# The first eight weights' words assembled in a PSUM bank instead of SBUF, in a one-core attention and gated-MLP kernel

## The chip, the cores and the metric

The kernel runs on one core of one Trainium2 chip. The metric is the device time of one execution in microseconds (us), median of several runs. TensorE is written PE, VectorE DVE, ScalarE ACT, GpSimd POOL, and SP is the engine that issues most transfers.

## The reference

The inputs arrive as float64-sized words for the weights and float32 for q, k and v. Three blocks follow one another:

```python
scores = scale * np.matmul(q_c, k_c.transpose(0, 1, 2, 4, 3))   # 64x64 chunks, softmax, times v
x = attention output as (B=8, S=576, 512)
h = np.maximum(x @ w_in, 0.0); u, v = h[..., :512], h[..., 512:]
v_s = np.einsum('ts,bsd->btd', w_spatial, layernorm(v)) + b_spatial[None, :, None]
x = (u * v_s) @ w_out
u = x + (x.transpose(0, 2, 1) @ U @ V).transpose(0, 2, 1)
out = u + np.maximum(u @ w_ch1, 0.0) @ w_ch2
```

## The kernel before, in words

**Layout.** Activations lie transposed. Nearly all matrix products are made with float16 pairs: each operand is split into a high and a low float16 part, and three matmuls (hi·hi, hi·lo, lo·hi; `mm3`, lines 149 to 152) accumulate in a PSUM bank. The attention is cut into 36 tiles of 128 rows; the gated block (`gen_moe`) goes once per batch, eight times; the channel block (`gen_ch`) goes over nine slices of 512 rows.

**The weights.** They come as 44 blocks of 128x512 eight-byte words and are unpacked on the chip, block n in these steps:

- `dec_load` (line 157) issues the transfer of the raw words, for the first eight blocks into buffers called `room` that other tiles use later.
- `dec_abs` (line 163) takes a float32 tile `dt` and has ACT write the scaled high words into it (line 173). Blocks under 12 use the SBUF tag `hid`, which has three buffers.
- `dec_bits` (line 176) works on `dt` in place with three DVE instructions over 128x512 elements: a shift (line 180, one tensor input), an OR with the shifted low words (line 181) and an OR with the sign bit (line 184). Lines 181 and 184 have two tensor inputs each, the raw words and `dt`.
- `dec_parts` (line 188) casts `dt` to the high float16 part on ACT (line 191), and POOL subtracts to make the low part (line 192). The `dt` buffer is free after that.

Blocks 4, 5, 6, 7 (the second half of `w_in`) and then 0, 1, 2, 3 (the first half) are unpacked first, by `gen_dec(0)`; `gen_dec(1)` then unpacks the spatial weights, blocks 8 to 11 and U and V. The other 32 blocks follow later between the other work.

**The opening.** `gen_first` does the first nine attention tiles in float32: scores (line 516), maximum, subtraction and exponential (lines 385 to 389), normalisation (lines 394 to 397), a transpose on PE (line 529), a copy on ACT (line 530), the product with v (line 537), and the split into float16 parts (`a_out`: line 410 on ACT, line 411 on DVE). PE also runs two groups of 16 matmuls whose results nobody uses, one on the tile `warm` (line 451) and one on `idle` (line 465). POOL clears some buffers with memsets (line 897 clears two of them), some of them after block 7 is unpacked. The gated block of batch 0 begins with products of the first attention rows with blocks 4 to 7.

**PSUM.** The pool `ps_h` has three banks with tag `h`. It serves the warm-up matmuls (`wp`), later every product of the gated block (`pb`) and the hidden rows of the channel block (`phid`). The opening's attention uses other banks.

**What sets the order.** The program is written as Python generators that are drained in a fixed order: tiles 0 to 4, then `gen_dec(0)`, `gen_dec(1)`, then batch 0 with parts of batch 1. When the program is built, a scheduler lays the instructions of every engine into one queue, by its own estimate of when each one's inputs and buffers are ready, and puts in the waits. On the chip each engine takes its queue strictly in that order. So a buffer that is thought free earlier can move an instruction in the queue.

Of the kernel before, what the change touches and what calls it, by code (L numbers as in the profile page):

```python
# [8 lines left out]
F32 = mybir.dt.float32  # L9
F16 = mybir.dt.float16  # L10
U32 = mybir.dt.uint32
I64 = mybir.dt.int64
ACTF = mybir.ActivationFunctionType
ALU = mybir.AluOpType
# [87 lines left out]
def moe_kernel(  # L102
# [16 lines left out]
    sb = ctx.enter_context(tc.tile_pool(name="sb", bufs=1))  # L119
    ps_acc = ctx.enter_context(tc.tile_pool(name="ps_acc", bufs=1, space=PSUM))  # L120
    ps_h = ctx.enter_context(tc.tile_pool(name="ps_h", bufs=3, space=PSUM))
# [33 lines left out]
    stage = {}  # L155
# [6 lines left out]

    def dec_abs(name, g=None):
        st, cols = stage[name]
        if isinstance(name, int) and name < 12:
            t = sb.tile([128, 2, 512], F16, tag="hid", name="dt", bufs=3)
            t = t.rearrange("p a n -> p (a n)").bitcast(F32)
        else:
            t = sb.tile([128, 512], F32, tag="o", name="dt", bufs=2)
        if g is not None:  # L170
            nc.scalar.copy(out=t[0:1, 0:1], in_=g[0:1, 0:1])  # L171
        hi = st[:, 0:cols].bitcast(U32)[:, 1::2]
        nc.scalar.activation(out=t[:, 0:cols], in_=hi.bitcast(F32), func=ACTF.Copy, scale=W_SC)
        stage[name] = (st, cols, t)

    def dec_bits(name):
        st, cols, t = stage[name]
        w = st[:, 0:cols].bitcast(U32)
        tb = t[:, 0:cols].bitcast(U32)
        nc.vector.tensor_scalar(out=tb, in0=tb, scalar1=3, scalar2=None, op0=ALU.logical_shift_left)  # L180
        nc.vector.scalar_tensor_tensor(  # L181
            out=tb, in0=w[:, 0::2], scalar=29, in1=tb, op0=ALU.logical_shift_right, op1=ALU.bitwise_or
        )
        nc.vector.scalar_tensor_tensor(  # L184
            out=tb, in0=w[:, 1::2], scalar=0x80000000, in1=tb, op0=ALU.bitwise_and, op1=ALU.bitwise_or
        )

    def dec_parts(name):
# [67 lines left out]
    def gen_dec(part):  # L256
# [17 lines left out]
        def run(names, loaded=False, step=1700.0):  # L274
            n = len(names)
            for i in range(-1, n + 2):
                if i + 1 < n and not loaded:
                    ld(names[i + 1])
                if 0 <= i < n:
                    dec_abs(names[i])  # L280
                if 0 <= i - 1 < n:
                    dec_bits(names[i - 1])
                    fin(names[i - 1])
                yield "wait", step
# [28 lines left out]
    def next_rest(g):  # L313
        i = given[1]
        load_rest(i + 1)
        n = late[i]
        dec_abs(n, g)
        if i == 11:
            load_rest(16, nc.sync)
        elif 12 <= i < 24:  # L320
            load_rest(min(i + 4, 24))
        dec_bits(n)
        dec_parts(n)
        given[1] += 1
# [674 lines left out]
```

## Time and profile before

| | |
|---|---|
| runs before, median (lowest to highest) | 1315.21 us (1314.82 to 1318.34) of 3 |
| span of the profiled execution | 1312.6 us |
| own time of the profiled execution | not listed apart from its span; the median lies 2.6 us above the span |
| busy share of the span: PE, DVE, ACT, POOL | 97%, 41%, 39%, 39% |
| DMA | 81.43 MB, 62 GB/s over the span |

The span runs from the first to the last instruction. An engine is busy while one of its instructions runs; an instruction that is held back after its start counts as busy too, so one kind of instruction at one shape can have very different durations. The idle time in front of an instruction is put down to what ended last before it.

### The profile page before, as it was taken

The page shows a single profiled execution, that of the slowest core. Times are in us where ns is not written, and L with a number is a line of the kernel's source. Part 1 is how long each engine was busy: PE and PEld are TensorE (multiplying, and loading weights), DVE is VectorE, ACT ScalarE, POOL GpSimd, SP SyncE. Part 2 cuts the span into 40 slices and gives each one's busy share as a digit, 9 for nine tenths or more (in the row PEclk, how much of TensorE's full clock was granted, in tenths as well). Part 3 has the DMA queues.
Part 4 walks back from the last instruction along what each step waited for, and adds up shares of the span by engine and source line. Part 5 has one row for each costly group of instructions (what it writes and reads, how often), then busy time and mean ns, then how long its engine had stood idle before and what let it go on. Part 6 is the DMA issues. An engine that isn't in the chain of part 4 may idle for free.

```text
span 1312.6 us, 20572 instructions
## 1 busy us (share of the span) xinstructions
PE 1270.3 (97%) x8324; PEld 727.5 (55%) x8324; DVE 532.3 (41%) x946; ACT 517.3 (39%) x1062; POOL 518.4 (39%) x644
## 2 busy tenths in 40 slices
PE   7899888899999999999999999999999999999998
PEld 5677455445666556654665456645655565544443
DVE  7975787655343533334134514242113211221211
ACT  7865566545545433533344424323122212221110
POOL 7654877656555454534155415223111311020000
PEclk7889999899999999999999999999999999999999
DMA  8644353432224311321024101210011001000000
GB/s 283 194 150 109 104 169 97 136 88 79 61 65 74 92 33 42 75 51 41 4 68 91 49 1 33 40 37 5 0 27 36 8 0 28 18 24 1 32 0 32
DMA packets 99015, 81.43 MB, mean 62 GB/s; under 512 B 73828, under 2 KB 74468, under 8 KB 98920
## 3 DMA queue, kind: packets, MB, share of 16 engines
q1 hardware_dynamic: 97768, 75.92, 21.2%
q10 hardware_dynamic: 1152, 4.19, 1.0%
q8 instruction: 65, 1.06, 0.3%
q14 instruction: 30, 0.25, 0.1%
HBM read 53.62 MB, written 9.44 MB: 48 GB/s over the span
## 4 chain that ended last, share of the span: by engine, by line
PE 73%; DVE 8%; DMA 7%; ACT 6%; POOL 4%; issue 3%; SPq 0%; DVEq 0%; ACTq 0%; POOLq 0%
PE acc L150 8%; PE acc L152 8%; PE acc L151 8%; PE phid L151 8%; PE phid L150 8%; PE phid L152 8%; PE pb L150 7%; PE pb L152 7%; PE pb L151 7%; DMA pt<-ph 2%; DVE dt L184 2%; DMA vf<-in_v_dram 2%; DVE dt L181 1%; DMA st<-in_wk_dram 1%; POOL vbd L376 1%
## 5 line engine op out<-in xcount | busy, mean ns | idle before, releaser
L830 DVE SCALAR_TENSOR_TENSOR hid<-phid,hid 128x512 f16<-128x512 f32 x144 | 99.2, 689 | 383.5 <-ACT hid L828 383.2
L150 PE MATMUL phid<-uT,wch 128*128 128x512 f16 x576 | 219.3, 381 | 0.0
L152 PE MATMUL phid<-uT,wch 128*128 128x512 f16 x576 | 219.1, 380 | 0.0
L151 PE MATMUL phid<-uT,wch 128*128 128x512 f16 x576 | 219.1, 380 | 0.0
L151 PE MATMUL acc<-hid,wch 128*128 128x512 f16 x576 | 218.6, 379 | 0.2 <-DVE hid L830 0.2
L152 PE MATMUL acc<-hid,wch 128*128 128x512 f16 x576 | 218.6, 379 | 0.0
L150 PE MATMUL acc<-hid,wch 128*128 128x512 f16 x576 | 208.1, 379 | 0.7 <-ACT hid L828 0.7
L152 PEld LDWEIGHTS <-wch 128*128 128x128 f16 x1152 | 112.9, 98 | 132.8 <-issue 1.8
L150 PEld LDWEIGHTS <-wch 128*128 128x128 f16 x1152 | 112.9, 98 | 120.3 <-issue 4.5
L151 PEld LDWEIGHTS <-wch 128*128 128x128 f16 x1152 | 113.0, 98 | 116.0 <-issue 1.0
L828 ACT ACTIVATE hid<-phid 128x512 f16<-128x512 f32 x144 | 85.5, 594 | 176.6 <-PE phid L152 175.5
L376 POOL TENSOR_TENSOR vbd<-vf,vbd 64x512 f16<-64x512 f32 x54 | 65.0, 1204 | 113.1 <-ACT vbd L375 99.2
L702 POOL TENSOR_TENSOR gt<-g,gt 128x288 f16<-128x288 f32 x64 | 50.4, 789 | 137.0 <-ACT gt L700 136.6
L363 POOL TENSOR_TENSOR qbd<-qk,qbd 64x512 f16<-64x512 f32 x54 | 64.5, 1195 | 46.9 <-ACT qbd L362 44.9
L751 POOL TENSOR_TENSOR uT<-x,uT 128x512 f16<-128x512 f32 (+7 forms) x64 | 47.7, 756 | 89.4 <-ACT uT L750 86.5
L768 POOL TENSOR_TENSOR tr<-x,tr 128x64 f16<-128x64 f32 x64 | 47.5, 763 | 86.8 <-issue 47.1
L150 PE MATMUL pb<-gt,w 128*128 128x288 f16 x256 | 72.9, 286 | 3.8 <-ACT dt L171 1.9
L150 PE MATMUL pb<-sp_m,vn 128*128 128x288 f16 x256 | 73.5, 287 | 2.9 <-DVE g L697 2.9
L151 PE MATMUL pb<-xT,w 128*128 128x288 f16 x256 | 74.5, 291 | 0.0
L152 PE MATMUL pb<-xT,w 128*128 128x288 f16 x256 | 74.4, 290 | 0.0
L150 PE MATMUL pb<-xT,w 128*128 128x288 f16 x256 | 74.3, 291 | 0.0
L151 PE MATMUL pb<-sp_m,vn 128*128 128x288 f16 x256 | 73.6, 287 | 0.0
(179 smaller groups left out, 2343.9 us busy)
## 6 DMA issues: line engine op xcount, KB each, us to landing
st<-in_wk_dram SPq DMA_DIRECT2D x24, 512.0 KB, 3.6
out_dram<-ot SPq DMA_DIRECT2D x32, 256.0 KB, 2.1
vf<-in_v_dram SPq DMA_DIRECT2D x27, 256.0 KB, 2.7
qk<-in_q_dram SPq DMA_DIRECT2D x27, 256.0 KB, 2.7
qk<-in_k_dram SPq DMA_DIRECT2D x27, 256.0 KB, 3.0
room<-in_wk_dram SPq DMA_DIRECT2D x8, 512.0 KB, 7.2
wch<-in_wk_dram ACTq DMA_DIRECT2D x8, 512.0 KB, 3.2
wch<-in_k_dram SPq DMA_DIRECT2D x9, 256.0 KB, 2.9
```

The costliest lines, as they stand in the source:

```text
L150: nc.tensor.matmul(out=o, lhsT=wh, rhs=xh, start=start, stop=False)
L151: nc.tensor.matmul(out=o, lhsT=wh, rhs=xl, start=False, stop=False)
L152: nc.tensor.matmul(out=o, lhsT=wl, rhs=xh, start=False, stop=stop)
L181: nc.vector.scalar_tensor_tensor(out=tb, in0=w[:, 0::2], scalar=29, in1=tb, op0=ALU.logical_shift_right, op1=ALU.bitwise_or)
L184: nc.vector.scalar_tensor_tensor(out=tb, in0=w[:, 1::2], scalar=0x80000000, in1=tb, op0=ALU.bitwise_and, op1=ALU.bitwise_or)
L363: nc.gpsimd.tensor_tensor(out=qbd[r, 1, :, c, :], in0=qv[r], in1=qbd[r, 0, :, c, :], op=ALU.subtract)
L376: nc.gpsimd.tensor_tensor(out=vbd[r, 1, :, :, c, :], in0=vf[r], in1=vbd[r, 0, :, :, c, :], op=ALU.subtract)
L702: nc.gpsimd.tensor_tensor(out=gt[:, 1, m, c], in0=g, in1=gt[:, 0, m, c], op=ALU.subtract)
L751: nc.gpsimd.tensor_tensor(out=buf[:, 1, m, c], in0=x2[:, m, t], in1=buf[:, 0, m, c], op=ALU.subtract)
L768: nc.gpsimd.tensor_tensor(out=th[:, o0:o0 + n], in0=x2[:, m, t0:t0 + n], in1=th[:, t0:t0 + n], op=ALU.subtract)
L828: nc.scalar.activation(out=hd[:, 0, :], in_=p, func=ACTF.Relu)
L830: nc.vector.scalar_tensor_tensor(out=hd[:, 1, :], in0=p, scalar=0.0, in1=hd[:, 0, :], op0=ALU.max, op1=ALU.subtract)
```

## The change

For blocks under 8, `dec_abs` now takes `dt` from the PSUM tag `h` (a bank of the gated block), and the first two DVE instructions work there in place. The third writes its result into a tile of the SBUF tag `hid`, which is taken only then, and which ACT and POOL read as before. Blocks 8 to 11 and all others stay as they are.

```diff
     def dec_abs(name, g=None):
         st, cols = stage[name]
-        if isinstance(name, int) and name < 12:
+        if isinstance(name, int) and name < 8:
+            t = ps_h.tile([128, 512], F32, tag="h", name="dp")
+        elif isinstance(name, int) and name < 12:
             t = sb.tile([128, 2, 512], F16, tag="hid", name="dt", bufs=3)
             t = t.rearrange("p a n -> p (a n)").bitcast(F32)
         else:
...
         nc.vector.scalar_tensor_tensor(
             out=tb, in0=w[:, 0::2], scalar=29, in1=tb, op0=ALU.logical_shift_right, op1=ALU.bitwise_or
         )
+        to = tb
+        if isinstance(name, int) and name < 8:
+            t = sb.tile([128, 2, 512], F16, tag="hid", name="dt", bufs=3)
+            t = t.rearrange("p a n -> p (a n)").bitcast(F32)
+            to = t[:, 0:cols].bitcast(U32)
+            stage[name] = (st, cols, t)
         nc.vector.scalar_tensor_tensor(
-            out=tb, in0=w[:, 1::2], scalar=0x80000000, in1=tb, op0=ALU.bitwise_and, op1=ALU.bitwise_or
+            out=to, in0=w[:, 1::2], scalar=0x80000000, in1=tb, op0=ALU.bitwise_and, op1=ALU.bitwise_or
         )
```

## Rows read from the trace of the kernel before

**Rows 1.** The page: busy time of PE, and PE's granted clock in 40 slices.

```profile
PE 1270.3 (97%) x8324; PEld 727.5 (55%) x8324; DVE 532.3 (41%) x946; ACT 517.3 (39%) x1062; POOL 518.4 (39%) x644
...
PEclk7889999899999999999999999999999999999999
```

**Rows 2.** Busy time by stretch: us, engines in turn, granted clock, DMA share, GB/s.

```profile
0.00:40.00 40.00, 33.26 (x164) 23.92 (x164) 30.38 (x57) 31.88 (x55) 28.57 (x28) 0.79 0.78 270
40.00:80.00 40.00, 35.64 (x212) 25.83 (x212) 39.09 (x81) 29.79 (x60) 22.93 (x32) 0.83 0.57 181
300.00:600.00 300.00, 298.97 (x2247) 173.09 (x2245) 124.88 (x232) 137.59 (x278) 149.66 (x184) 1.00 0.26 65
```

**Rows 3.** DVE's groups from 7 to 40 us: count, busy us, mean ns, idle before.

```profile
L181 DVE SCALAR_TENSOR_TENSOR dt<-room,dt 128x512 uint32<-128x512 uint32 x8 | 6.8, 846 | 0.1
L184 DVE SCALAR_TENSOR_TENSOR dt<-room,dt 128x512 uint32<-128x512 uint32 x8 | 6.6, 821 | 0.1
L180 DVE TENSOR_SCALAR dt<-dt 128x512 uint32<-128x512 uint32 x8 | 4.9, 615 | 6.9 <-ACT dt L173 6.8
L385 DVE TENSOR_REDUCE mx<-sp 128x8 f32<-128x512 f32 x4 | 2.7, 680 | 0.0
```

**Rows 4.** Timeline of DVE: start, duration in us, instruction, idle before and its releaser.

```profile
9.00 0.69 DVE L184 SCALAR_TENSOR_TENSOR dt<-room,dt 128x512 uint32<-128x512 uint32 x1
9.79 0.43 DVE L180 TENSOR_SCALAR dt<-dt 128x512 uint32<-128x512 uint32 x1
...
25.60 1.31 DVE L180 TENSOR_SCALAR dt<-dt 128x512 uint32<-128x512 uint32 x1
26.83 0.67 DVE L184 SCALAR_TENSOR_TENSOR dt<-room,dt 128x512 uint32<-128x512 uint32 x1
...
29.24 1.09 DVE L184 SCALAR_TENSOR_TENSOR dt<-room,dt 128x512 uint32<-128x512 uint32 x1
33.30 0.68 DVE L180 TENSOR_SCALAR dt<-dt 128x512 uint32<-128x512 uint32 x1 [2.97 <-ACT dt L173]
34.01 1.65 DVE L181 SCALAR_TENSOR_TENSOR dt<-room,dt 128x512 uint32<-128x512 uint32 x1
35.58 0.68 DVE L385 TENSOR_REDUCE mx<-sp 128x8 f32<-128x512 f32 x1
```

**Rows 5.** Timeline of POOL.

```profile
24.81 1.82 POOL L897 MEMSET qbd<- 128x2048 f16 x1
...
28.62 3.83 POOL L192 TENSOR_TENSOR w<-dt,w 128x512 f16<-128x512 f32 x3
32.41 2.69 POOL L232 TENSOR_TENSOR sp_m<-st,sp_m 128x576 f16<-128x576 f32 x2
```

**Rows 6.** Timeline of ACT.

```profile
30.36 0.62 ACT L191 CAST w<-dt 128x512 f16<-128x512 f32 x1 [1.04 <-DVE dt L184]
...
32.61 0.66 ACT L173 ACTIVATE dt<-room 128x512 f32<-128x512 f32 x1
...
38.53 0.57 ACT L652 ACTIVATE rz<-pb 128x512 f32<-128x512 f32 x1
```

**Rows 7.** Timeline of PE.

```profile
28.06 0.63 PE L150 MATMUL pb<-w,xT 128*128 128x512 f16 x1
...
38.21 1.95 PE L537 MATMUL of<-wch 128*128 128x64 f32 x16
41.87 0.39 PE L150 MATMUL pb<-w,xT 128*128 128x512 f16 x1 [1.71 <-ACT xT L410]
...
43.44 1.09 PE L529 MATMUL tp<-ident,wch 128*128 128x128 f32 x4 [0.97 <-DVE wch L397]
```

**Rows 8.** Busy time by stretch, as in rows 2, for two short ones.

```profile
44.00:48.00 4.00, 4.00 (x12) 1.63 (x11) 3.71 (x5) 3.48 (x6) 3.77 (x5) 0.50 0.50 197
66.00:74.00 8.00, 7.99 (x38) 6.21 (x38) 8.00 (x27) 4.97 (x13) 3.59 (x6) 0.57 0.51 169
```

**Rows 9.** Waits of the SP queue, 0 to 100 us: total us, times, longest.

```profile
SPq L160 <- DVE dt L184: 18.7, 7, 9.0
```

## The prediction

> **What bounds the kernel now.** First the page: PE is busy 97% of the span, and its granted clock stays at 0.9 or more outside the first slices and one later one [rows 1]. The stretches then say where PE is short of work. From 300 to 600 us it is busy 298.97 of 300 us at full clock, so nothing that DVE does there can help; in the first 80 us it is busy 68.9 us, at 0.79 and 0.83 of its clock [rows 2]. The eight unpackings lie in the first 40 us. After them, from 40 to 80 us, DVE is busy 39.09 of 40 us [rows 2]: there every microsecond of DVE work saved or moved forward counts, up to what PE can take. PE's fixed work follows behind the opening, so a shift of the opening passes through to the end almost whole.
>
> In the groups of DVE, the three instructions of the eight unpackings take 6.8 + 6.6 + 4.9 = 18.3 us [rows 3]. In the timeline the two-input ones take 0.67 to 0.69 us when undisturbed, the shift 0.43 us; but single ones take 1.31, 1.09 and 1.65 us [rows 4]. Beside each of the long ones POOL has an instruction running: a memset from 24.81 to 26.63, subtractions from 28.62 to 32.45, further ones from 32.41 to 35.1 [rows 5].
>
> The second thing to see is a hole. DVE stands 2.97 us before the shift of the eighth block at 33.30, waiting for ACT's line 173, which began only at 32.61 [rows 4, 6]. Behind that shift, in DVE's queue, stands the maximum of an attention tile (line 385 at 35.58), whose softmax ends in the transpose on PE at 43.44 [rows 4, 7]. ACT for its part had stood 1.04 us before 30.36 for the stretched line 184 [rows 6]. PE then has gaps of 1.71 us before 41.87 and 0.97 us before 43.44 [rows 7]. After them its granted clock is 0.50, the lower of its two levels (1.2 against 2.4 GHz), from 44 to 48 us, with no idle time in that stretch [rows 8].
>
> **The change part by part.**
>
> *The shift, line 180.* It now reads and writes PSUM. Undisturbed it takes 0.43 us in SBUF; DVE's other single-input pass over 128x512 words, the reduction of line 385, reads PSUM and takes 0.680 [rows 3, 4]. I take the slower, 0.69, since PSUM is what it shares with line 385: 8 x 0.69 = 5.5 us against 4.9 now, a loss of 0.6. The lower end is 8 x 0.43 = 3.4, a gain of 1.5. The Trainium skill speaks against the change here: "VectorE: DVE Perf Modes", in "Why PSUM operands drop a tier", says that a PSUM operand takes from such an instruction the mode that reads with both SBUF ports. By it the sum has the loss of 0.6; without it, the gain of 1.5. No run here shows a shift in PSUM.
>
> *The two ORs, lines 181 and 184.* One of their two tensor inputs leaves SBUF. If the stretching beside POOL ends, each costs its undisturbed 0.69: 5.5 us each, against 6.8 and 6.6, a gain of 1.3 and 1.1. If it stays, nothing is gained. The skill's "SBUF — State Buffer", in "Who interferes with whom", says that a DVE instruction with two SBUF inputs contends with a POOL instruction that reads SBUF, and one with at most one such input does not. The long rows beside POOL agree with its first half; of the second half no row tells. By it the gain is whole. No row shows DVE writing PSUM. Above, I bound all three instructions by 0.85, the mean of line 181 as it stands: 24 x 0.85 = 20.4 us, 2.1 more than now.
>
> Sum on DVE: 18.3 - 16.5 = 1.8 us less.
>
> *ACT's line 173.* It writes PSUM instead of SBUF. It takes 0.66 now; ACT reading PSUM at this size takes 0.57 [rows 6]. Eight times 0.09 is 0.7 us to gain at most; since no reason excludes a loss, I allow as much upward, and take none. ACT is busy 31.88 of 40 us, which covers most of it [rows 2].
>
> *The buffers.* This is the larger part. Before, a `hid` buffer was held from line 173 to POOL's line 192. The eighth block needed the fifth one's, whose line 192 is the first of three from 28.62, so done about 29.9, after POOL's memsets [rows 5]. With `dt` in PSUM, line 173 of block eight waits only for a bank, free after line 184 of an earlier block; the sixth one's ended at 27.5 [rows 4]. So ACT can do it before its other work, and the hole of 2.97 us closes but for the new wait: line 184 now takes the `hid` buffer, and for the eighth block still needs the one free at 29.9. Block seven ends at 30.33 now, about 28.5 without the stretches; the eighth's first two steps add 1.2 us; 0.2 to 0.4 of waiting are left. I take 2.97 - 0.4 = 2.6 us.
>
> *PSUM banks.* Three banks are shared with `pb`. The warm-up and eight word tiles come before the first `pb`; taken in turn, it needs the bank of the sixth block, free at 27.5, for its matmul at 28.06 [rows 4, 7]. So 0.5 us cover it; if that is gone, PE waits by as much as line 184 is late.
>
> *SP.* No transfer moves by itself. SP stands 18.7 us in seven waits for line 184 before loads on line 160 [rows 9]; loads that wait for one of the eight can go earlier, and their landing is not what PE waits for in rows 7. I cost it at nothing; cover gone, a load late by a DVE step costs that step, under 1 us.
>
> *The sum.* DVE gains 1.8 + 2.6 = 4.4 us before the saturated stretch. What PE can take: its gaps, 1.71 + 0.97 = 2.7 us, and, if these go and the clock does not fall after them, half of the 4 us at 0.50 and half of the 1.09 us transpose: 2.5 us. That is 5.2 us, more than DVE gives, so DVE decides: 4.4 us. The profiled execution spans 1312.6 us, and 2.6 more make the median of 1315.2: I forecast 1315.2 - 4.4 = 1310.8 us. From 0.3%, or 3.9 us, on a measurement can tell it from no change.
>
> **The rivals.**
>
> *Only the stretches go.* The scheduler leaves line 173 of block eight behind the spatial weights' casts on ACT. For it: ACT's queue is full there. Against: its buffer was what was late. DVE then saves 1.8 us: 1313.4.
>
> *The stretches stay.* What holds the ORs is not their second SBUF input, or POOL holds PSUM work as well. The shift loses 0.6 and the hole closes by little: 1315.8. Against it: undisturbed rows of one line agree within 0.02 us, and only those beside POOL are long [rows 4, 5].
>
> *The wait moves to DVE, and the kernel is slower.* Line 184 of block eight takes the place of line 173 as the one that waits for POOL. Before, ACT's wait left DVE's queue free to pass tiles that stood ahead. If the three steps of block eight now stand at about 27 us in DVE's queue, line 184 stands there until 29.9, with a normalisation and a split of the attention behind it: a stall of 2.9 us, which PE sees as a gap. Another stretch at half clock like the one of rows 8 costs 2.5; half of the saving of 1.8 comes off: 2.9 + 2.5 - 0.9 = 4.5 us, 1319.7. It decides once line 184 stands more than about 2.5 us ahead of POOL. For it: POOL comes to line 192 of block five only at 28.62 [rows 5]. Against it: the scheduler lays POOL's queue too, memsets included, and has other work to put ahead.
>
> **How the numbers follow.** The forecast case gets 0.46, the stretches alone 0.25, the wait on DVE 0.21, stretches that stay 0.08. The forecast case has a range of its own: with gaps gone but the clock still falling it gives 2.7 us (1312.5; 0.04 of the 0.46). At best PE takes all its 5.2, and the later fall, 8 us at 0.57 from 66 to 74 [rows 8], goes too, worth 3.4: 8.6 us, 1306.6. So faster by over 0.3% gets 0.42, within it 0.04 + 0.25 + 0.08 = 0.37, slower 0.21. The range runs from 1306.6 to 1319.8, to just past the slower case; the bound of DVE's unknown price, 2.1 us up, lies inside it.
>
> **What would show it.** Right: lines 181 and 184 of the eight at 0.69 each with POOL busy beside them; the shift at 0.69; the wait of about 3 us before an eighth shift gone, and the maximum of the third tile some 4 us before 35.58; the gaps near 40 to 43 us smaller, and the clock at full after them. Wrong: an idle DVE, or a long line 184, ended by POOL's line 192; ORs still over 1 us beside POOL; or the same gaps and half-clock stretch a little later.

## The result, and the profile after

The changed kernel takes 1323.73 us (median of 6 runs, 1322.22 to 1329.01), the kernel before 1316.24 us in the same comparison (6 runs, 1314.82 to 1318.34). The ratio is 1.0055, with a 95% interval of 1.004 to 1.007: **slower by some 7 us**, where 1310.8 was forecast, and outside the range. The profiled execution took 1323.86 us and spans 1322.1, against 1312.6 before.

Line numbers are 2 to 8 higher than before: the shift is line 182, the ORs are 183 and 192, the cast is 199, the split of an attention tile is 418 on ACT. First the page, PE and its clock in 40 slices, to be held against [rows 1]:

```profile
PE 1271.6 (96%) x8324; PEld 729.5 (55%) x8324; DVE 535.1 (40%) x946; ACT 517.5 (39%) x1062; POOL 513.3 (39%) x644
...
PEclk7799899999999999999999999999999999999999
```

PE is busy 1.3 us longer in a span that is 9.5 us longer, so most of the time went into gaps. The stretches (columns as in [rows 2]) of the changed kernel:

```profile
0.00:40.00 40.00, 33.09 (x161) 24.11 (x162) 29.53 (x60) 32.62 (x57) 30.31 (x30) 0.79 0.83 285
40.00:80.00 40.00, 33.21 (x186) 23.87 (x186) 36.13 (x75) 27.44 (x56) 19.98 (x31) 0.79 0.55 159
300.00:450.00 150.00, 145.35 (x1164) 85.46 (x1161) 63.31 (x115) 72.14 (x144) 81.18 (x99) 1.00 0.28 68
```

and the last of these stretches in the kernel before:

```profile
300.00:450.00 150.00, 149.40 (x1167) 87.23 (x1164) 64.86 (x121) 74.48 (x149) 85.84 (x103) 1.00 0.30 73
```

From 40 to 80 us DVE is busy 3.0 us less than before [rows 2]. It is not relieved, it is short of work: PE did 186 matmuls there instead of 212. And PE lost another 4 us from 300 to 450, hundreds of microseconds after the last instruction that the diff touches.

The steps that the diff does touch did what was expected. DVE's groups from 7 to 40 us, against [rows 3]:

```profile
L182 DVE TENSOR_SCALAR dp<-dp 128x512 uint32<-128x512 uint32 x8 | 5.6, 696 | 2.6 <-ACT dp L175 2.6
L183 DVE SCALAR_TENSOR_TENSOR dp<-room,dp 128x512 uint32<-128x512 uint32 x8 | 5.4, 681 | 0.0
L192 DVE SCALAR_TENSOR_TENSOR dt<-room,dp 128x512 uint32<-128x512 uint32 x8 | 5.4, 679 | 0.2
```

Together they take 16.4 us, where 16.5 was forecast and 18.3 stood before. The timeline of DVE, against [rows 4]:

```profile
27.42 0.68 DVE L183 SCALAR_TENSOR_TENSOR dp<-room,dp 128x512 uint32<-128x512 uint32 x1
28.21 0.69 DVE L192 SCALAR_TENSOR_TENSOR dt<-room,dp 128x512 uint32<-128x512 uint32 x1
31.97 0.69 DVE L393 TENSOR_REDUCE mx<-sp 128x8 f32<-128x512 f32 x1 [3.07 <-PE sp L524]
32.70 0.69 DVE L396 TENSOR_TENSOR wch<-sp,mx 128x512 f32<-128x512 f32 x1
35.57 0.69 DVE L402 TENSOR_REDUCE sm<-wch 128x8 f32<-128x512 f32 x1 [2.18 <-ACT wch L397]
```

The eight blocks are done at 28.9 us. Before, the last OR of the eighth ran to 36.9:

```profile
36.18 0.69 DVE L184 SCALAR_TENSOR_TENSOR dt<-room,dt 128x512 uint32<-128x512 uint32 x1
```

The maximum of the third tile comes at 31.97 instead of 35.58. So DVE won its time, and then stood 3.07 us for PE's scores and 2.18 us for ACT's exponential. ACT's timeline, and then PE's, with its two longest gaps up to 66 us:

```profile
39.74 0.69 ACT L237 ACTIVATE st<-st 128x576 f32<-128x576 f32 x1 [2.49 <-DMA st<-in_wsp_dram]
...
44.83 0.58 ACT L418 CAST xT<-of 128x512 f16<-128x512 f32 x1
```

```profile
37.66 1.95 PE L545 MATMUL of<-wch 128*128 128x64 f32 x16
...
45.47 0.61 PE L150 MATMUL pb<-w,xT 128*128 128x512 f16 x1 [4.57 <-ACT xT L418]
...
63.93 0.47 PE L150 MATMUL pb<-w,xT 128*128 128x512 f16 x1 [2.10 <-ACT xT L418]
```

PE had finished the second tile's product (`of`) at 39.6. Its split, line 418, stands in ACT's queue behind a step of a spatial weight (line 237), whose transfer was issued at 33.73 and took 5.9 us, and behind seven more instructions. PE waits 4.57 us for it; before, the gap at this place was 1.71 us, and the same split ran at 41.23. Behind the gap PE's granted clock stays at the lower level for longer than before, where it was 0.50 from 44 to 48 us [rows 8] and 0.85 from 48 to 52:

```profile
44.00:48.00 4.00, 2.40 (x9) 1.50 (x9) 3.94 (x8) 3.48 (x7) 3.71 (x5) 0.50 0.28 54
48.00:52.00 4.00, 4.00 (x18) 3.35 (x18) 3.48 (x9) 1.64 (x4) 0.69 (x4) 0.50 0.83 259
```

All queues have been laid anew: the rows of PE, DVE, ACT, POOL and SP stand in another order, ACT's and DVE's from about 10 us on, the others' from about 30. PE, DVE, ACT and POOL have their last difference between 475 and 490 us, SP at 314; behind that the order is the old one. The program has the same number of instructions on every engine.

To see where the time goes I use one sum for all kernels: the time elapsed less what PE's matmuls begun by then take at full clock (0.213 us for one of 512 float16 columns, 0.107 us for one of 64 float32 columns, which is the spacing of their starts where the clock is full, and others in proportion to their columns). It is the time that PE has lost, by standing or by half clock, in each profiled execution:

| us lost by PE | 0 to 70 | 70 to 300 | 300 to 450 | 450 to 1300 |
|---|---|---|---|---|
| before | 26.1 | 37.3 | 3.9 | 16.8 |
| changed | 30.3 | 38.9 | 8.4 | 15.9 |

These are single executions. The three kernels of the old order (before, psum_old_order and own_buffers_old_order below) lose 26.1 to 26.5 us up to 70 us and 3.9 to 4.2 us from 300 to 450, but 37.3 to 40.8 us from 70 to 300. So in the second column a difference of 3 us says nothing about the order.

### The profile page after: what moved, and what is told of

Its sections match the earlier page's. It is cut to its first block, busy times and chain, and to the rows that moved or that the text cites. A ratio compares the mean times of both kernels' runs of the same rounds, so it can differ in the third digit from the quotient of the medians.

```text
span 1322.1 us, 20572 instructions
## 1 busy us (share of the span) xinstructions
PE 1271.6 (96%) x8324; PEld 729.5 (55%) x8324; DVE 535.1 (40%) x946; ACT 517.5 (39%) x1062; POOL 513.3 (39%) x644
## 3 DMA queue, kind: packets, MB, share of 16 engines
q1 hardware_dynamic: 97768, 75.92, 21.1%
## 4 chain that ended last, share of the span: by engine, by line
PE 71%; DVE 8%; DMA 6%; POOL 6%; ACT 6%; issue 3%; SPq 0%; DVEq 0%; POOLq 0%; ACTq 0%
PE acc L152 8%; PE phid L151 8%; PE phid L150 8%; PE phid L152 8%; PE acc L151 8%; PE acc L150 8%; PE pb L150 6%; PE pb L152 6%; PE pb L151 6%; DMA pt<-ph 2%; DMA vf<-in_v_dram 2%; DVE dt L192 1%; POOL vbd L384 1%; DVE dt L183 1%; POOL wch L200 1%
## 5 line engine op out<-in xcount | busy, mean ns | idle before, releaser
L150 PE MATMUL pb<-gt,w 128*128 128x288 f16 x256 | 73.6, 288 | 4.1 <-DVE hid L838 4.1
L150 PE MATMUL pb<-sp_m,vn 128*128 128x288 f16 x256 | 73.2, 286 | 1.5 <-DVE g L705 1.5
L151 PE MATMUL pb<-gt,w 128*128 128x288 f16 x256 | 73.5, 288 | 0.0
```

The lines of the kernel that those rows point to most:

```text
L150: nc.tensor.matmul(out=o, lhsT=wh, rhs=xh, start=start, stop=False)
L151: nc.tensor.matmul(out=o, lhsT=wh, rhs=xl, start=False, stop=False)
```

## The experiments

**How an order was forced.** The scheduler keeps any order that dependencies demand. In the runs below, unless said otherwise, each engine's instructions are tied to a given order by dependencies of the scheduler alone, with both ends on one engine and no semaphore; SP's issues are tied as well. In the traces of these runs every engine's rows stand in the order asked for. At the old order the tying costs nothing that can be told (own_buffers_old_order below, ratio 0.9997); at the new order it was not measured by itself. Lines of these kernels are 8 higher again. The code, shortened:

```diff
+    for e, order in ORDER.items():          # one list for each engine
+        for x, y in zip(order, order[1:]):
+            tc.add_manual_dep(traced[e][y], traced[e][x].name, NoSync)
```

**1. The old order with the words in PSUM (psum_old_order), and the new order with the words in SBUF (sbuf_new_order).** The first is the changed kernel with the order of the kernel before, the second the kernel before with the order of the changed one.

> The words stand in PSUM as in the changed kernel, but every engine's queue is pinned to the order of the kernel before. Theory A (the new order of the queues costs the time): 1313 to 1317 us, as the kernel before or 1 to 2 us under it, with the stretched ORs gone. Theory B (the words in PSUM cost it: a slower shift, banks shared with the gated block): 1321 to 1325 us, as the changed kernel.

> The words stand in SBUF as before, but every queue is pinned to the order of the changed kernel. Theory A: 1321 to 1327 us, as the changed kernel or a little worse, since the fourth word tile must now wait on ACT for a buffer in an order that was made for free banks. Theory B: 1314 to 1318 us, as the kernel before.

Measured: 1318.28 us, ratio 1.0014 (1.0003 to 1.0025), and 1327.76 us, ratio 1.0096 (1.0069 to 1.0124). The first lies 1.3 us above the range of theory A and 2.7 under that of B, the second 0.8 us above that of A. With the change, but not its order, nearly all of the loss is gone; with the order, but not the change, it is there in full and more. The lost time shows it at the same places: 26.3 and 4.2 us (0 to 70 and 300 to 450 us) in the first, 32.7 and 7.7 in the second.

In the old order the rows of the three steps are not shorter with the words in PSUM: 18.4 us, against 18.3 before. DVE's groups from 7 to 40 us in psum_old_order:

```profile
L191 DVE SCALAR_TENSOR_TENSOR dp<-room,dp 128x512 uint32<-128x512 uint32 x8 | 6.5, 811 | 0.1
L200 DVE SCALAR_TENSOR_TENSOR dt<-room,dp 128x512 uint32<-128x512 uint32 x8 | 6.4, 798 | 0.1
L190 DVE TENSOR_SCALAR dp<-dp 128x512 uint32<-128x512 uint32 x8 | 5.5, 688 | 7.2 <-ACT dp L183 7.2
...
L411 DVE TENSOR_SCALAR sm<-sm 128x8 f32<-128x8 f32 x2 | 2.4, 1184 | 0.0
L413 DVE TENSOR_TENSOR wch<-wch,sm 128x512 f32<-128x512 f32 x2 | 2.3, 1154 | 0.0
```

and two ORs that are still long, in the timeline of DVE and then of POOL:

```profile
24.11 1.75 DVE L411 TENSOR_SCALAR sm<-sm 128x8 f32<-128x8 f32 x1
24.18 1.68 DVE L200 SCALAR_TENSOR_TENSOR dt<-room,dp 128x512 uint32<-128x512 uint32 x1
24.78 1.67 DVE L191 SCALAR_TENSOR_TENSOR dp<-room,dp 128x512 uint32<-128x512 uint32 x1
```

```profile
24.03 1.80 POOL L913 MEMSET qbd<- 128x2048 f16 x1
```

The instruction that POOL's memset holds is now one of the softmax, over 8 elements, whose operands are in SBUF; it takes 1.75 us and ends with the memset (25.86 and 25.83), and the two ORs queue behind it. The Trainium skill, "SBUF — State Buffer", in "Who interferes with whom", says that a DVE instruction in a mode that uses both port pairs and a POOL instruction lock each other out for the whole of one of them, and that a DVE instruction with at most one SBUF input outside such modes is free of it. This small instruction agrees with the first half. The ORs at 27.42 and 28.21 in the changed kernel, 0.68 and 0.69 us beside two subtractions of POOL, agree with the second:

```profile
26.95 2.27 POOL L200 TENSOR_TENSOR w<-dt,w 128x512 f16<-128x512 f32 x2
```

At the new order, on the other hand, the three steps are short without PSUM too. Their groups in sbuf_new_order (lines 181, 184 and 180 of the kernel before), with the words in SBUF:

```profile
L189 DVE SCALAR_TENSOR_TENSOR dt<-room,dt 128x512 uint32<-128x512 uint32 x8 | 5.7, 716 | 0.0
L192 DVE SCALAR_TENSOR_TENSOR dt<-room,dt 128x512 uint32<-128x512 uint32 x8 | 5.4, 682 | 0.1
L188 DVE TENSOR_SCALAR dt<-dt 128x512 uint32<-128x512 uint32 x8 | 5.0, 623 | 6.6 <-ACT dt L181 6.6
```

That is 16.1 us, against 16.4 in the changed kernel; in own_buffers_new_order below, again in SBUF, it is 17.2. So most of the changed kernel's gain on these steps, or all of it, comes with the order: what POOL does beside an OR depends on it.

**2. Which stretch of the order costs (old_opening_new_rest, new_opening_old_rest).** The words in PSUM; each queue up to 120 us in one order, and then in the other.

> Words in PSUM; the queues follow the kernel before for what it starts in its first 120 us, and the changed kernel's order for the rest. Theory A split in two: the opening's order costs about 4 us and the later order about 5; here the later part alone, 1319 to 1322 us. If the opening alone is at fault: 1314 to 1317 us. Theory B: 1321 to 1325.

> Words in PSUM; the queues follow the changed kernel for what it starts in its first 120 us, and the order of the kernel before for the rest. Theory A split in two: the opening alone, 1318 to 1321 us, with PE's gap of 4.6 us before the split of the second attention tile. If the opening alone is at fault: 1321 to 1325 us. Theory B: 1321 to 1325.

Measured: 1322.98 us, ratio 1.0049 (1.0032 to 1.0065), and 1328.18 us, ratio 1.01 (1.0073 to 1.0127). The lost time by stretch is 25.6, 40.2, 7.7, 16.3 us in the first and 32.0, 49.5, 4.1, 17.1 us in the second. The opening loses where it is the new one, and 300 to 450 us where the rest is the new one. The halves do not add up, though. The second is 7 us above its range, and by the ratios the two cost 0.49% and 1.0%, where the whole new order costs 0.55%. Its 49.5 us from 70 to 300 are more than in any other kernel here; part of that is chance, since the profiled execution, 1333.21 us, is the slowest of its four. What waits there was not followed; the two orders may not fit where they are joined.

**3. Is it the one split on ACT (split_ahead, splits_and_copy_ahead)?** The changed kernel's order; in the first, the split of the second tile stands ahead of the spatial weight that waits for its transfer; in the second, two more steps of the chain stand ahead, ACT's copy of the third tile's transposed scores and DVE's part of the split.

```diff
-ACT: ... 67 (spatial weight, waits for its load) ... 27 (split of the second tile) ...
+ACT: ... 27 67 ...
```

> The changed kernel in its own pinned order, but ACT's split of the second attention tile stands in front of the spatial block whose load is late, instead of eight instructions behind it. Theory C (ACT's queue, standing for that load, is what costs the opening): PE's gap of 4.6 us near 41 to 45 us shrinks to under 1 us and 1 to 4 us of the 7 are won: 1320 to 1323 us. Rival D (the gap is due to PE's or DVE's work and only moves): 1323 to 1325, with another gap of like size behind it.

> As the run before, and also ACT's copy of the third tile's transposed scores and DVE's half of the second tile's split stand in front of the spatial work. Theory C: the whole loss of the opening, about 4 us, is won back: 1318.5 to 1321 us. Rival D: no better than 1323.

Measured: 1325.69 us, ratio 1.0064 (1.0042 to 1.0087), and 1325.76 us, 1.0064 (1.004 to 1.0087). Neither is better than the changed kernel, and both lie above what was expected if ACT's queue were the cause. PE's gap is still there, behind another step each time. PE in split_ahead:

```profile
48.83 3.67 PE L553 MATMUL of<-wch 128*128 128x64 f32 x16 [5.20 <-ACT wch L546]
...
66.52 0.61 PE L158 MATMUL pb<-w,xT 128*128 128x512 f16 x1 [2.47 <-ACT xT L426]
```

and in splits_and_copy_ahead:

```profile
42.52 2.00 PE L553 MATMUL of<-wch 128*128 128x64 f32 x16 [1.18 <-ACT wch L546]
...
49.16 1.09 PE L545 MATMUL tp<-ident,wch 128*128 128x128 f32 x4 [4.65 <-DVE wch L413]
...
64.11 0.61 PE L158 MATMUL pb<-w,xT 128*128 128x512 f16 x1 [2.74 <-ACT xT L426]
```

So the wait that the profile names was not by itself the cause: the chain of an attention tile goes through PE, DVE, ACT and PE again, and with one link moved ahead the next one was late in both runs. What would make the whole chain early in this order is not shown.

**4. Mending the stretch from 300 us (old_order_from_300, both_mended).** The changed kernel's order up to 300 us, then the old one; in the second also the moves of splits_and_copy_ahead.

> The changed kernel in its own pinned order for what it starts in its first 300 us, then the order of the kernel before. Theory E (the later order of the changed kernel loses 4 us more than the old one between 300 and 450 us, where PE stands for the transposes of the softmax): 1318.5 to 1321 us. Rival F (those waits follow from the lateness of the opening, whatever the order): 1323 to 1325 us.

> Both edits: the opening with the three instructions ahead, and the old order from 300 us on. Theories C and E together: 1314.5 to 1317.5 us, level with the kernel before. If one of them fails: 1318.5 to 1321 us.

Measured: 1326.05 us, ratio 1.0055 (1.0034 to 1.0076), and 1327.79 us, 1.0083 (1.006 to 1.0105). Both miss what was expected of them. From 300 to 450 us they lose 9.8 and 9.4 us, no less than the 8.4 of the changed kernel. Rival F, that the lateness of the opening does this, is out as well: in new_opening_old_rest, with the old order from 120 us on behind the same new opening, this stretch loses 4.1 us. So the order from 120 to 300 us has a part in it. What the new order loses there is at least named by the waits of PE from 300 to 450 us, in the changed kernel and then in the kernel before:

```profile
PE o L150 <- DMA pt<-ph: 4.6, 4, 1.8
```

```profile
PE o L150 <- DMA pt<-ph: 0.5, 1, 0.5
```

The late transfers are the transposes of later attention tiles (`pt`). Two other traces, one of each order, agree: 4.3 us in own_buffers_new_order, 0.4 in own_buffers_old_order. Why the transfers are late in this order was not found.

**5. PSUM or the order: the words in buffers of their own (sbuf_words_own_buffers, own_buffers_new_order, own_buffers_old_order).** sbuf_new_order left a doubt: there the words still held the `hid` buffer, so its waits are not the changed kernel's. Here the words lie in two SBUF buffers of their own, and `hid` is taken by the third DVE step alone, as in the changed kernel. The first leaves the order to the scheduler, the other two tie it to that of the changed kernel and to the old one.

```diff
-            t = ps_h.tile([128, 512], F32, tag="h", name="dp")
+            t = sb.tile([128, 512], F32, tag="o", name="dp", bufs=2)
```

> The words of the eight blocks in SBUF, in two buffers of their own (shared with the output's tiles later), with the hid buffer taken only by the third DVE step, as in the changed kernel. Nothing is in PSUM, and the scheduler lays the queues as it likes. If the freed hid buffer is what made the new order and the new order is what costs: the queues come out near the changed kernel's, the opening (to 70 us) loses 4 to 6 us more than before, and the time is 1321 to 1328. If PSUM itself were the cost: 1313 to 1317, no slower than before.

> The words in two SBUF buffers of their own, as in sbuf_words_own_buffers, and every queue in the order of the changed kernel (1323.7 us). Nothing is in PSUM, and no hid buffer is held over the three DVE steps. If the order is the cost: 1322 to 1326, the opening to 70 us loses 4 to 6 us more than before's 26, and PE stands for the ACT split of the second tile near 45 us. If a part of the cost was PSUM: that part is missing, 1316 to 1320.

> The same words in SBUF buffers of their own, and every queue in the order of the kernel before. With the words in PSUM this order took 1318.3 (1.0014 of before). If PSUM is what costs the 0.14%: 1316 to 1317, level with before. If it is chance or the freed buffer: 1318, as with PSUM.

Measured: 1319.53 us, ratio 1.0017 (1.0003 to 1.0032); 1326.84 us, 1.0076 (1.0046 to 1.0105); and 1316.91 us, 0.9997 (0.9978 to 1.0016). The second is the clearest run of the study: no word in PSUM, `hid` taken as in the changed kernel, its order, and the whole loss (0.8 us above the range expected). It loses 32.8 us up to 70 us and 7.9 from 300 to 450. The third says that at the old order nothing is lost; its interval and psum_old_order's overlap, so whether PSUM costs the 0.14% there is open.

The first run missed its expectation in part. The freed `hid` buffer alone, with nothing in PSUM, does make the scheduler lay every queue anew, and the result is slower than before. But it is a third order, not the changed kernel's: its rows differ from those of the kernel before only between 22 and 114 us. Its opening loses 25.3 us, as little as before, and its 300 to 450 us 4.2. Where it loses its 0.17% is not shown: the 40.9 us that it loses from 70 to 300 us are 40.8 in own_buffers_old_order, which is level with the kernel before.

At the old order DVE can be compared with and without PSUM. The same groups as under 1, in own_buffers_old_order:

```profile
L191 DVE SCALAR_TENSOR_TENSOR dp<-room,dp 128x512 uint32<-128x512 uint32 x8 | 6.8, 847 | 0.1
L200 DVE SCALAR_TENSOR_TENSOR dt<-room,dp 128x512 uint32<-128x512 uint32 x8 | 6.6, 819 | 0.1
L190 DVE TENSOR_SCALAR dp<-dp 128x512 uint32<-128x512 uint32 x8 | 4.5, 563 | 7.3 <-ACT dp L183 7.3
...
L411 DVE TENSOR_SCALAR sm<-sm 128x8 f32<-128x8 f32 x2 | 1.8, 902 | 0.0
L413 DVE TENSOR_TENSOR wch<-wch,sm 128x512 f32<-128x512 f32 x2 | 1.4, 680 | 0.0
```

PSUM takes 0.5 us off the ORs, adds 1.0 to the shift and 1.5 to the softmax steps, which now meet POOL instead. The sums, 21.1 us with the words in SBUF and 23.1 with them in PSUM, are not DVE's time, though: rows that wait behind one another cover the same moments, as the three from 24.11 do. With each moment counted once, DVE is busy 26.00 of the 33 us with the words in PSUM, and 26.35 without; psum_old_order first, then own_buffers_old_order, columns as in [rows 2]:

```profile
7.00:40.00 33.00, 26.68 (x143) 20.25 (x142) 26.00 (x51) 28.04 (x50) 19.89 (x18) 0.74 0.77 274
7.00:40.00 33.00, 25.17 (x144) 19.36 (x143) 26.35 (x51) 28.23 (x50) 21.98 (x18) 0.79 0.77 273
```

So at this order PSUM moves DVE's long rows to other instructions and gives it next to nothing.

**6. The step that the forecast rested on (eighth_word_ahead, eighth_word_and_softmax_ahead, own_buffers_softmax_ahead, sbuf_old_order_softmax_ahead).** The forecast's 2.6 us were to come from ACT doing the first step of block eight earlier. In the first run this is the only move in the old order, with the words in PSUM. In the second, the third tile's exponential and the second tile's split stand ahead on ACT as well. The third has this order with the words in SBUF buffers of their own. The fourth is the kernel before with the two softmax moves alone.

```diff
-ACT: ... 59 61 57 60 63 62 56 (first step of block eight) ...
+ACT: ... 56 59 61 57 60 63 62 ...
-ACT: ... 64 58 65 28 (exponential) 92 66 67 203 68 27 (split) ...
+ACT: ... 28 64 58 65 92 66 67 27 203 68 ...
```

> The words in PSUM, every queue in the order of the kernel before (as psum_old_order, 1318.3 us), but ACT's first step of the eighth block stands six places further ahead, before the spatial weights. If the late first step of the eighth block holds the opening back, as the prediction took it: DVE's wait of 2.9 us before the eighth shift closes to under 0.5, the maximum of the third tile comes about 1.4 us earlier (then PE's scores hold it, which end at 33.8), and the time falls by 1 to 2 us, 1316.3 to 1317.3. If that wait was cover (ACT's queue holds the exponential behind the same other work whatever DVE does): DVE's wait closes and opens again behind ACT, the exponential of the third tile stays at 38.7, and the time stays at 1318.3, within 1 us.

> As eighth_word_ahead, and two further steps on ACT stand ahead of work that nobody waits for: the exponential of the third tile (ahead of three spatial and unpacking steps) and the split of the second tile's output (ahead of a block-diagonal part of V). If ACT's order on the chain is what costs in the opening: the exponential at about 37.0 us instead of 38.7, the gap of 1.9 us on PE before 42.6 falls to under 1, and the time falls by 2 to 3 us against psum_old_order, 1315.3 to 1316.3. If any move by hand lets another step of the chain come late, as in split_ahead, the gap turns up in another place and the time stays at 1318 or rises.

> The same words in SBUF buffers of their own, and the order of eighth_word_and_softmax_ahead (1316.5 with PSUM, 1.0002 of before). If PSUM costs some 2 us at any order: 1314 to 1315, faster than before. If not: 1316.5, within 1 us.

> The words in SBUF (the kernel before), every queue in its own order but for the same two steps on ACT: the exponential of the third tile and the split of the second tile's output stand ahead. If ACT's order on the chain costs in the opening: the gap of 1.7 us on PE before 41.9 falls under 1 and the time by 1 to 2 us, 1314 to 1315. If gaps only move: 1316, within 1 us, or above.

Measured: 1317.6 us, ratio 1.0005 (0.9992 to 1.0018); 1316.54 us, 1.0002 (0.9988 to 1.0015); 1317.71 us, 1.0001 (0.9984 to 1.0018); 1315.38 us, 0.9989 (0.9973 to 1.0005). DVE in eighth_word_ahead:

```profile
30.03 0.68 DVE L190 TENSOR_SCALAR dp<-dp 128x512 uint32<-128x512 uint32 x1
30.75 0.69 DVE L191 SCALAR_TENSOR_TENSOR dp<-room,dp 128x512 uint32<-128x512 uint32 x1
...
32.89 0.69 DVE L401 TENSOR_REDUCE mx<-sp 128x8 f32<-128x512 f32 x1 [1.45 <-PE sp L532]
...
37.85 0.69 DVE L410 TENSOR_REDUCE sm<-wch 128x8 f32<-128x512 f32 x1 [3.08 <-ACT wch L405]
```

The hole before the eighth shift is closed, as forecast. Half of it opens again at once before the maximum, which waits for PE's scores, and 0.9 us more before the sum (3.08 against 2.17 us in psum_old_order), since the exponential stands behind other work in ACT's queue. By the ratios (1.0005 against 1.0014) the time is some 1.2 us better than psum_old_order's, and the intervals overlap, so it may be nothing. With the exponential moved too, it comes at 35.03 instead of 37.21. PE in eighth_word_and_softmax_ahead, its gaps alone:

```profile
40.23 0.39 PE L158 MATMUL pb<-w,xT 128*128 128x512 f16 x1 [0.68 <-ACT xT L426]
...
44.97 1.08 PE L532 MATMUL sp<-wch 128*128 128x64 f32 x8 [1.49 <-issue]
...
50.14 0.63 PE L545 MATMUL tp<-ident,wch 128*128 128x128 f32 x4 [1.42 <-DVE wch L413]
...
52.23 3.57 PE L553 MATMUL of<-wch 128*128 128x64 f32 x16 [1.03 <-ACT wch L546]
```

Of the gap of 1.94 us that psum_old_order has before 42.59, 0.68 us is left, and gaps of 1.0 to 1.5 us come behind it, up to 52 us. The time is level with the kernel before, and own_buffers_softmax_ahead, the same order without PSUM, is level with it too (1.0001 against 1.0002): here PSUM is not seen to cost anything. Of these four, none can be told from it; the last has a median 1.6 us under before's, with an interval that still holds 1.

## Why the prediction was wrong

**The step that failed** is the premise of the sum: that the change moves line 173 of block eight and leaves the rest of the queues as they were. The text on the kernel before says that a buffer thought free earlier can move an instruction. Here instructions moved on every engine, up to some 490 us. Every other term was priced in the old order, and the new one costs PE 4.2 us in the opening, 1.6 from 70 to 300 us (within what profiles of one order differ by there) and 4.5 from 300 to 450 and gives back 0.9 behind (the table above): 9.4 us between the profiled executions, 7.5 in the medians. That the order is the cost, and not PSUM, is shown by own_buffers_new_order and psum_old_order together. Which part of the change draws this order, the freed `hid` or the banks taken, is open, since `hid` freed by itself drew another. Why this order is worse at each place is shown only in part, by the waits it ends in.

**"DVE decides"** failed with it. The sum took DVE, busy 39.09 of 40 us behind the opening, for what holds PE there. In the changed kernel DVE had its gain on the three steps and an earlier maximum, was busy 36.13 us in that stretch, and PE did 26 matmuls fewer in it.

**The slower rival** got its sign right and its mechanism wrong. The third step of block eight does not wait for POOL; it runs at 28.21 for 0.69 us. The gap that PE sees is behind ACT's queue, and moving ACT's split out of it did not help. That the time came out slower, as this rival said, is luck. The two rivals between had the old order in their sums, as the forecast had.

**The shift** was sized right: 0.70 us forecast as 0.69, against 0.43 in SBUF. The rule of the Trainium skill that was weighed there ("VectorE: DVE Perf Modes", "Why PSUM operands drop a tier") agrees with this.

**The ORs** were sized right for the changed kernel, 0.68 each. But the gain of 1.8 us on the three steps is no property of PSUM. At the new order they take 16.1 or 17.2 us with the words in SBUF. At the old order they take 18.4 us with the words in PSUM: the shift costs 0.6 us more, and the ORs win 0.5 us of the 2.4 forecast, since two of them stand behind a small softmax step that POOL holds. "If the stretching ends" should have read: if POOL then finds no other DVE instruction in front of them to hold. And of the three long rows that were set beside POOL's, the one at 25.60 is no OR but a shift [rows 4].

**The hole of 2.97 us** was worth less than 2.6 us. The maximum behind it needs the third tile's scores, and PE ends these at 33.28 in the kernel before, its group of 16 from 29.77 for 3.51 us; so at most 2.3 us could reach the maximum. The group in the kernel before:

```profile
29.77 3.51 PE L516 MATMUL sp<-wch 128*128 128x64 f32 x16
```

Behind that, ACT came to the exponential at 38.01 after work without a gap since 30.36, so an earlier maximum could not bring it forward by as much. eighth_word_ahead puts the whole step at about 1 us, if at anything, and shows two waits that take the hole's place, PE's scores and ACT's queue.

**SP at nothing** rests on "No transfer moves by itself", which holds for the diff and not for a queue laid anew: SP's issues moved too, and the load that ACT stood 2.49 us for is one of them. No run puts a price on it; in split_ahead the split no longer stood behind that load, and the time stayed.

**PSUM banks** and ACT's line 173 were rightly priced at nothing: of PE's and ACT's waits from 20 to 50 us in the changed kernel, none names a bank or an unpacking step for more than 0.3 us.

## What to carry to other kernels

Where a scheduler lays the queues, an edit that frees or takes a buffer is two changes: its own, and a new order, which here reached some 490 us into the program from an edit whose last instruction ends at 28.9. The second can be larger, and no row of the trace before prices it; tie the old order and measure the two apart before believing that the edit is good or bad. And price a closed hole by what the instruction behind it waits for next, on every engine of its chain, before counting it as time gained.

## What was not expected of the hardware

A DVE instruction over 128x8 elements, with all its operands in SBUF, took 1.75 us beside a POOL memset of 1.80 us, and 0.28 us for another tile in eighth_word_and_softmax_ahead. So a short instruction can be held as long as a long one, and two ORs behind it ended 1.0 us late with it (1.68 and 1.67 us).

Two orders do not add up by their parts: with the old order from 120 us on, behind the new opening, the time was 1.0% over the kernel before, where the whole new order costs 0.55% and the whole old order with PSUM 0.14%.
